# An FFT mixer and an FFN on one core: 47-point steps spread between 64-point steps, weight sums moved to POOL alone in chunks five and six

## The chip, the cores and the metric

One core of a Trainium2 chip runs the whole program. The metric is the device time of one execution in microseconds (us), the median of several runs. The engines are named as in the profile: PE multiplies matrices (PEld loads its weights), DVE and POOL do elementwise work, ACT copies and evaluates functions, SP issues most DMAs. Each engine runs its own instructions in order and waits in order. Tiles are 128 partitions high; POOL works on SBUF alone, and PE's results land in PSUM.

## The reference

```python
X = np.fft.rfft(x, axis=1)                   # x: (8, 3008, 256), real
Xr, Xi = X.real, X.imag
Yr = soft(Xr @ w_r - Xi @ w_i + b_r)         # soft(v) = sign(v) * max(|v| - 0.01, 0)
Yi = soft(Xr @ w_i + Xi @ w_r + b_i)
y = np.fft.irfft(Yr + 1j * Yi, n=3008, axis=1)
t = y.reshape(8 * 3008, 256)                 # 24064 tokens
out = (sigmoid(t @ w_gate) * (t @ w_val)) @ w_out    # d_ff = 1536
```

## The kernel before

**The FFT.** 3008 = 47 x 64. For each batch the forward transform is a 47-point step (`fwd_a`: load x, multiply by `fa`, store z to DRAM), then 64-point steps. A 64-point step `step(q, b)` holds three stages of neighbouring q: `fwd_b` multiplies z by `mf` (tile `pb`), `mix` applies `w_r` and `w_i` (tiles `pm`, then `yt`, `ys`, `yc`), and `inv_b` multiplies by `mi_sb` (tile `pi`) and stores v to DRAM. An inverse unit `inv_a` loads v (tile `vf`), multiplies by `fb` (tile `pia`), and leaves tokens in SBUF for the first nine chunks or writes them to DRAM (`yf` to `yd`). Batches stand in five groups of 1, 1, 2, 2, 2. The 47-point work of batch 0 and 1 comes first, that of the third group (`half_a`) beside chunk 0. Products are made from a rounded part and a rest (`xh` and `xl`, `yh` and `yl`, `hh` and `hl`), so most come as three matmuls.

**The FFN.** Chunks of 512 tokens and 12 units of 128 hidden channels: `ffn1` gives `pg` and `pv` (12 matmuls), then `sg`, `hh`, `hl`, and `ffn2` adds to `po` (6 matmuls). Chunks 0 to 8 run like this, 108 units. The remaining 19 pairs of chunks use a Strassen form with seven products in place of eight, written out by hand under a manual schedule. It needs sums of weight blocks: `make_t` computes them (tiles `tb` and `tr`) and stores them in `td`; `load_t` and `load_t1` bring them back as `th`, `tl` and into `w1h`, `w1l` before the Strassen part.

**What sets the order.** Beside the units of chunks 1 to 8 runs a list `side` of all other steps, each with a weight. Each FFN unit adds `rate` to a sum, and steps are taken from the list while the sum covers their weight. Before, `side` goes group by group: the 64-point steps of group 1; those of group 2 with the inverse units of group 1 spread among them; then for each of the last two groups all its 47-point steps, then its 64-point steps, with the inverse units of the group before spread over both; at last the inverse units of the last group. The result goes through a scheduler that gives each engine a fixed order by priority, readiness and free slots, so that an instruction may stand far ahead of its place in the code. Slots come from rings named by tag: `big` (x, z, raw weights, `tb`, `tr`), `r2k` (rounded parts), `vf` (v).

**Names that the prediction uses.** `xl` L179 is the rest of x, on POOL in `fwd_a` and on DVE in `half_a`; `xh` L178 its rounded part on ACT; `mi_sb` L221 the load of the inverse matrices, issued by POOL; `tr` L495 the copy of the sums on ACT; `hl` L381 the rest of the hidden values on DVE.

Of the kernel before, what the change touches and what calls it, by code (L numbers as in the profile page):

```python
# [9 lines left out]
F32 = mybir.dt.float32  # L10
F32R = mybir.dt.float32r
# [8 lines left out]
R2, R1 = 47, 64  # L20
NK2 = 24
NQ = 2 * NK2
# [4 lines left out]
HW = 512  # L27
FFT_BANKS, L1_BANKS, L2_BANKS = 3, 3, 2

NF2K, NR2K, NLD, NST, NBIG, NME, NVF, NHH, NSG, NYF = 5, 5, 3, 3, 5, 2, 3, 3, 2, 2  # L30
NCB, NTMP, NHP = 10, 9, 12

SIDE_GAP = 14
PRE = 4
WARM = 24
EARLY = 8
NCONV = 5
# [69 lines left out]
def tile_fft_mix_ffn(ctx: ExitStack, tc, x, w_r, w_i, b_r, b_i, w_one, w_out, mf, mi, mis, fa, fa32, fb, out):  # L107
    nc = tc.nc
    B, S, D = x.shape
    P = 128  # L110
# [11 lines left out]
    sub = nc.vector.tensor_sub  # L122
# [8 lines left out]
    p2 = fft.enter_context(tc.tile_pool(name="p2", bufs=2))  # L131
# [4 lines left out]
    def bank(name, tag="fft", bufs=FFT_BANKS):  # L136
        return (psf if tag == "fft" else psl).tile([P, 512], F32, tag=tag, bufs=bufs, name=name)
# [1 line left out]
    def f2k(name):  # L139
        return p2.tile([P, 2, D], F32, tag="f2k", bufs=NF2K, name=name)  # L140

    def r2k(name):
        return p2.tile([P, 2, D], F32R, tag="r2k", bufs=NR2K, name=name)

    fa_sb = cw.tile([2 * R2, 2, 2 * NQ], F32R, name="fa_sb")
    fa32_sb = cw.tile([2 * R2, 2 * NQ], F32, name="fa32_sb")
# [20 lines left out]
            nc.sync.dma_start(xf[lo_:hi_], xv[b, lo_:hi_, 4 * h:4 * h + 4])  # L167
        held["x", b, h] = xf

    def product_a(xi, az, whole, copy, sub_=nc.gpsimd.tensor_sub):  # L170

        pa = bank("pa")[:2 * NQ]
        if whole:
            nc.tensor.matmul(pa, fa32_sb, xi, start=True, stop=True)
        else:
            xh = r2k("xh")[:2 * R2]
            xl = r2k("xl")[:2 * R2]
            nc.scalar.copy(xh, xi)  # L178
            sub_(xl, xi, xh)  # L179
            nc.tensor.matmul(pa, fa_sb[:, 0], xh, start=True, stop=False)  # L180
            nc.tensor.matmul(pa, fa_sb[:, 0], xl, start=False, stop=False)
            nc.tensor.matmul(pa, fa_sb[:, 1], xh, start=False, stop=True)
        copy(az, pa.rearrange("p (h c) -> p h c", h=2))
# [15 lines left out]
    def half_a(b, h, whole):  # L199

        if ("xh", b, h) in held:
            xi = held.pop(("xh", b, h))[:2 * R2]
        else:
            xi = held["x", b, h // 2][:2 * R2, h % 2 * 2:h % 2 * 2 + 2]
        az = p2.tile([P, 2, D], F32, tag="st", bufs=NST, name="azh")[:2 * NQ]
        product_a(xi, az, whole, nc.scalar.copy, sub)
        nc.sync.dma_start(zv[b][:, 2 * h:2 * h + 2], az)


    def load_mf(q):  # L210
# [103 lines left out]


    def load_v(u):
        vf = p3.tile([P, 2, D], F32, tag="vf", bufs=NVF, name="vf")[:2 * NQ]
        b, h = divmod(2 * u, H)
        nc.sync.dma_start(vf, vv[b][:, h:h + 2])
        held["v", u] = vf  # L320
# [79 lines left out]
    def fft_units(bs, full=False):  # L400


        aa = [(b, h) for b in bs for h in range(R1 // 8)]
        ms = {}
        units = []

        def step_a(i):
            if i == 0:
                for k in range(min(PRE, len(aa))):
                    load_a(*aa[k])  # L410
            if i + PRE < len(aa):
                load_a(*aa[i + PRE])
            fwd_a(*aa[i])

        def loads(q, b):
            if b == bs[0]:
                if q == 0:
                    ms[0, 0] = load_mf(0)
                if q + 1 < NP:
                    ms[q + 1, 0] = load_mf(q + 1)  # L420
                if 0 <= q - 1 < NP:
                    ms[q - 1, 1] = load_mi(q - 1, full)
            if q == 0:
                load_b(b, 0)
            if q + 1 < NP:
                load_b(b, q + 1)

        def step(q, b):
            if q or not full:
                loads(q, b)  # L430
            if q < NP:
                fwd_b(b, q, ms[q, 0], full)
            if 0 <= q - 1 < NP:
                (mix4 if full else mix)(b, q - 1)
            if 0 <= q - 2 < NP:
# [47 lines left out]
    def make_t(fp, i):  # L483
        f0, f1 = 2 * fp, 2 * fp + 1
        g = nc.gpsimd
        w = big("tb").rearrange("p (a b) n -> p a b n", a=2)
        b, t = (w[:, a].rearrange("p a (b n) -> p a b n", b=2) for a in range(2))
        g.tensor_add(b, w1h[:, f0:f1 + 1, i], w1l[:, f0:f1 + 1, i])
        t = t.rearrange("p a b n -> p (a b) n")
        g.tensor_sub(t[:, 0], b[:, 1, 0], b[:, 0, 0])  # L490
        g.tensor_sub(t[:, 2], b[:, 1, 1], b[:, 1, 0])
        g.tensor_add(t[:, 1], t[:, 2], b[:, 0, 0])
        g.tensor_sub(t[:, 3], b[:, 0, 1], t[:, 1])
        r = p2.tile([P, 2, 4, P], F32R, tag="big", bufs=NBIG, name="tr")
        nc.scalar.copy(r[:, 0], t)  # L495
        g.tensor_sub(r[:, 1], t, r[:, 0])
        nc.gpsimd.dma_start(td[fp, i].rearrange("p (v a n) -> p v a n", v=2, a=4), r.bitcast(F32))

    def load_t(fp):
# [186 lines left out]
    groups, b0 = [], 0  # L686
# [13 lines left out]
    w1h = const.tile([P, NF, 2, CT, P], F32R, name="w1h")  # L700
    w1l = const.tile([P, NF, 2, CT, P], F32R, name="w1l")
# [73 lines left out]
    second_fft = fft_units(groups[1])[1]  # L775
    third_fft = fft_units(groups[2])[1]
# [24 lines left out]
    p3 = p3s.enter_context(tc.tile_pool(name="p3", bufs=2, side="right", reuse_waits="tile"))  # L801
    load_a(1, na - 1)
    for u in own0:
        load_v(u)
# [11 lines left out]

    side = []
    behind = []  # L820
    for g in groups[1:] + [[]]:
        main = []
        if g:
            main = second_fft if g is groups[1] else third_fft if g is groups[2] else sum(fft_units(g), [])
        m, n = len(main), len(behind)
        for i in range(m):
            side.append(main[i])
            side += behind[i * n // m:(i + 1) * n // m]
        if not g:
            side += behind  # L830
            behind_last = behind
        behind = []
        us = [u for b in g for u in range(b * H // 2, (b + 1) * H // 2) if u >= u0]
        for i, u in enumerate(us):
            def go(i=i, us=us):
                if i == 0:
                    load_v(us[0])
                if i + 1 < len(us):
                    load_v(us[i + 1])
                inv_a(us[i])  # L840
            behind.append((0.9, go))
    n_last = len(behind_last)
    end = len(ffn) - SIDE_GAP
    rate = sum(w for w, _ in side) / (end - NF)
# [1 line left out]
    p4 = None  # L846
    ts = [(fp, i) for fp in range(NH) for i in range(2)]
    for j, u in enumerate(ffn):
        c, f = divmod(j, NF)
        if c == 0:  # L850
            while raws and (f + 1) * nparts > (nparts - len(parts) - len(raws)) * (NF - 3):
                convert()
                if parts:
                    load_part()
        u()
        if c == 0:
            for i in range(f * nb // NF, (f + 1) * nb // NF):
                if i + 2 < nb:
                    load_half(*beside[i + 2])
                half_a(*beside[i], i % 2 == 0)  # L860
        else:
            acc += rate
            if ts and f % 2:
                make_t(*ts.pop(0))
        while side and (acc >= side[0][0] or j >= end):
            acc -= side[0][0]
            side.pop(0)[1]()
            if len(side) == n_last:
                fft.close()
                p4 = ctx.enter_context(tc.tile_pool(name="p4", bufs=1, reuse_waits="tile"))  # L870
                th, tl = (p4.tile([P, NH, 2, 3, P], F32R, name=t) for t in ("th", "tl"))
                prep = list(PREP)
                to_load = list(range(NH))
            if not side:
                psfs.close()
                psg = ctx.enter_context(tc.tile_pool(name="psg", bufs=1, space=bass.MemoryType.PSUM, reuse_waits="tile"))
        if p4 and to_load:
            load_t(to_load.pop(0))
        if c == NPL - 1:
            if f == 0:  # L880
                load_y(0)
# [21 lines left out]
    with tc.manual_schedule():  # L903
# [16 lines left out]
        n = NPR * NH  # L920
# [33 lines left out]
```

## Time and profile before

| | us |
|---|---|
| median of three runs | 2930.84 (2926.06 to 2931.66) |
| the profiled execution | 2931.34 |
| its span | 2929.6 |
| mean granted clock of PE | 0.979 |

| engine | busy us | share of the span | instructions |
|---|---|---|---|
| PE | 2855.9 | 97% | 13972 |
| PEld | 2351.8 | 80% | 13972 |
| DVE | 2074.0 | 71% | 3100 |
| ACT | 1356.6 | 46% | 2375 |
| POOL | 812.2 | 28% | 667 |

The first FFN unit starts at 124 us of the span, chunk 1 at 223 us, and the Strassen part at about 1180 us, from which on PE is busy without a break. The table gives sums over all stages; what each stage waits for is read from windows of the trace. A busy PE includes matmuls that run at half clock.

### The profile page before, as it was taken

How to read it: one execution, taken by the hardware profiler on the slowest of the kernel's cores; microseconds unless marked ns; L12 is line 12 of the kernel's file. 1: busy time of each engine (PE TensorE's matmuls, PEld its weight loads, DVE VectorE, ACT ScalarE, POOL GpSimd, SP SyncE). 2: the span in 40 equal slices, each digit the busy share in tenths (PEclk: the TensorE clock that was granted, in tenths of full speed). 3: DMA queues.
4: the chain of work that ended last, by engine and by line, in shares of the span. 5: the costliest groups of instructions: out<-in, count | busy, mean ns of one | idle time of the engine just before them, and what ended most of it. 6: DMA issues, size and time to landing. Idle time of an engine off the chain costs nothing.

```text
span 2929.6 us, 38731 instructions
## 1 busy us (share of the span) xinstructions
PE 2855.9 (97%) x13972; PEld 2351.8 (80%) x13972; DVE 2074.0 (71%) x3100; ACT 1356.6 (46%) x2375; POOL 812.2 (28%) x667
## 2 busy tenths in 40 slices
PE   8888999999999999999999999999999999999999
PEld 6656898789879977788888888888888888888887
DVE  4766987178539822677777777777777777777776
ACT  4554555545555533344444444444444444444443
POOL 0365001400230000233333333333333333333321
PEclk9889999999989998999999999999999999999999
DMA  9647544664564464000000000000000000000000
GB/s 268 196 158 225 143 129 124 188 186 137 152 197 143 131 196 125 12 29 30 15 15 29 29 29 15 15 29 30 29 15 15 29 29 30 15 15 29 29 15 15
DMA packets 177951, 237.43 MB, mean 81 GB/s; under 512 B 15682, under 2 KB 129152, under 8 KB 177760
## 3 DMA queue, kind: packets, MB, share of 16 engines
q1 hardware_dynamic: 162768, 215.98, 24.0%
q0 software_dynamic: 14896, 18.95, 2.5%
q8 instruction: 110, 1.80, 0.3%
q14 instruction: 81, 0.66, 0.1%
q10 hardware_dynamic: 96, 0.04, 0.0%
HBM read 133.72 MB, written 101.19 MB: 80 GB/s over the span
## 4 chain that ended last, share of the span: by engine, by line
PE 76%; DVE 3%; DMA 2%; issue 1%; ACT 1%; POOL 0%; SPq 0%; DVEq 0%; ACTq 0%; POOLq 0%
PE pd L613 11%; PE pc L613 11%; PE pa L613 11%; PE po L585 7%; PE po L584 7%; PE po L583 7%; PE pb L613 5%; PE pia L336 3%; PE pm L268 2%; DMA vf<-vd 1%; PE pb L234 1%; PE pg L371 1%; PE po L392 1%; PE po L390 1%; PE po L391 1%; PE pg L372 1%
## 5 line engine op out<-in xcount | busy, mean ns | idle before, releaser
L672 POOL TENSOR_TENSOR c<-c,c 128x512 f32<-128x512 f32 x114 | 147.2, 1291 | 810.8 <-DVE c L668 641.0
L585 PE MATMUL po<-hl,w 128*128 128x512 f32 x912 | 362.5, 398 | 0.0
L584 PE MATMUL po<-hh,w 128*128 128x512 f32 x912 | 361.6, 397 | 0.0
L583 PE MATMUL po<-hh,w 128*128 128x512 f32 x912 | 360.8, 396 | 0.0
L613 PE MATMUL pc<-s,w1h 128*128 128x512 f32 x912 | 284.1, 393 | 2.8 <-DVE v L647 2.8
L613 PE MATMUL pa<-a,w1h 128*128 128x512 f32 x912 | 284.6, 394 | 0.5 <-ACT u L639 0.5
L668 DVE TENSOR_TENSOR c<-u,pc 128x512 f32<-128x512 f32 x228 | 156.6, 687 | 115.6 <-PE pc L613 106.8
L643 DVE TENSOR_TENSOR u<-u,pb 128x512 f32<-128x512 f32 x228 | 155.3, 681 | 89.5 <-PE pb L613 62.8
L563 ACT CAST hh<-v 128x512 fp32r<-128x512 f32 x114 | 70.7, 620 | 306.2 <-DVE v L653 306.2
L585 PEld LDWEIGHTS po<-hl,w 128*128 128x128 f32 x912 | 171.5, 188 | 41.9
L583 PEld LDWEIGHTS po<-hh,w 128*128 128x128 f32 x912 | 172.0, 189 | 41.0
L613 PEld LDWEIGHTS pa<-a,w1h 128*128 128x128 f32 x912 | 171.4, 188 | 41.1 <-ACT u L639 0.9
L613 PEld LDWEIGHTS pc<-s,w1h 128*128 128x128 f32 x912 | 170.8, 188 | 41.3 <-DVE v L647 4.0
L567 POOL TENSOR_TENSOR hl<-c,hh 128x512 fp32r<-128x512 f32 x114 | 152.3, 1336 | 186.1 <-ACT hh L563 186.1
L584 PEld LDWEIGHTS po<-hh,w 128*128 128x128 f32 x912 | 171.0, 188 | 40.7
L377 DVE TENSOR_TENSOR sg<-sg,pv 128x512 f32<-128x512 f32 x108 | 74.2, 687 | 174.5 <-PE pv L373 165.0
L221 POOL DMA_DIRECT2D mi_sb<-in_mis_dram x48 | 34.1, 711 | 561.2 <-PE pi L307 527.2
L268 PE MATMUL pm<-w_sb,xsh 128*128 128x256 f32 x1008 | 188.9, 287 | 0.3 <-ACT xsh L250 0.2
L613 PE MATMUL pc<-s,w1l 128*128 128x512 f32 x456 | 177.5, 389 | 0.0
L613 PE MATMUL pa<-a,w1l 128*128 128x512 f32 x456 | 177.2, 389 | 0.0
L674 DVE TENSOR_TENSOR u<-u,pd 128x512 f32<-128x512 f32 x228 | 156.8, 688 | 24.9 <-DVE c L668 0.9
L645 DVE TENSOR_TENSOR v<-u,pd 128x512 f32<-128x512 f32 x228 | 156.8, 688 | 24.4 <-DVE u L643 0.5
(172 smaller groups left out, 7220.6 us busy)
## 6 DMA issues: line engine op xcount, KB each, us to landing
zf<-zd SPq DMA_DIRECT2D x96, 256.0 KB, 3.6
vd<-vz SPq DMA_DIRECT2D x96, 256.0 KB, 3.0
vf<-vd SPq DMA_DIRECT2D x128, 192.0 KB, 3.2
out_dram<-ot SPq DMA_DIRECT2D x94, 256.0 KB, 2.2
ypair<-yd SPq DMA_DIRECT2D x19, 1024.0 KB, 4.8
yd<-yf SPq DMA_DIRECT2D x103, 188.0 KB, 2.9
zd<-az SPq DMA_DIRECT2D x44, 384.0 KB, 3.6
xf<-in_x_dram SPq DMA_DIRECT2D x48, 256.0 KB, 4.3
```

The source lines that it names most:

```text
L268: nc.tensor.matmul(o, l, r, start=(i == 0), stop=(i == len(mms) - 1))
L336: nc.tensor.matmul(pa[:, ct, hh], vf[:, hh, ct * P:(ct + 1) * P], fb_sb[:, :PT], start=True, stop=True)
L567: sub_(hl, h, hh)
L583: nc.tensor.matmul(o, wh, hh, start=(f == 0), stop=False)
L584: nc.tensor.matmul(o, wl, hh, start=False, stop=False)
L585: nc.tensor.matmul(o, wh, hl, start=False, stop=(f == NF - 1))
L613: nc.tensor.matmul(o, l, r, start=not more and l is wh and r is xh, stop=l is wl, skip_group_check=more)
L643: add(u, u, b)
L645: add(v, u, d)
L668: add(c12, u, c)
L672: nc.gpsimd.tensor_mul(c12, g12, c12)
L674: add(u, u, d)
```

## The change

Five things change.

1. `side` is built by `merge`, which places each of several lists evenly between two points of a stretch. The first third of the 47-point steps of the fourth group goes between the 64-point steps of group 1 (from 20% on), the rest between those of the third group (up to 85%), and the 47-point steps of the fifth group between the 64-point steps of the fourth (up to 85%). Inverse units are spread as before, but with weight 0.65 in place of 0.9, so `rate` falls, and v is loaded two units ahead in place of one.
2. `make_t` has no ACT copy any more: POOL makes the rounded part itself, in halves. It is called in the odd units of chunks five and six, not from chunk one on.
3. `load_v` of the units that chunks 1 to 8 transform for themselves uses a slot of its own (`vo`), so the ring of three `vf` serves the others alone.
4. Rings: `r2k` 4 in place of 5 and two slots `a2k` for `xh` and `xl` of `fwd_a`; `big` 4 in place of 5; x is loaded two steps ahead in place of four.
5. `load_t` is called only when `side` is empty, in odd units.

```diff
-NF2K, NR2K, NLD, NST, NBIG, NME, NVF, NHH, NSG, NYF = 5, 5, 3, 3, 5, 2, 3, 3, 2, 2
-NCB, NTMP, NHP = 10, 9, 12
+NF2K, NR2K, NLD, NST, NBIG, NME, NVF, NVO, NHH, NSG, NYF = 5, 4, 3, 3, 4, 2, 3, 1, 3, 2, 2
+NCB, NTMP, NHP, NA2K = 10, 9, 12, 2
-PRE = 4
+PRE = 2
...
     def load_v(u):
-        vf = p3.tile([P, 2, D], F32, tag="vf", bufs=NVF, name="vf")[:2 * NQ]
+        own = 2 * UT <= u * UT < T0
+        vf = p3.tile([P, 2, D], F32, tag="vo" if own else "vf", bufs=NVO if own else NVF, name="vf")[:2 * NQ]
...
-        g.tensor_add(b, w1h[:, f0:f1 + 1, i], w1l[:, f0:f1 + 1, i])
+        for k, f in enumerate((f0, f1)):
+            g.tensor_add(b[:, k], w1h[:, f, i], w1l[:, f, i])
...
-        nc.scalar.copy(r[:, 0], t)
-        g.tensor_sub(r[:, 1], t, r[:, 0])
+        for k in (0, 2):
+            g.tensor_copy(r[:, 0, k:k + 2], t[:, k:k + 2])
+            g.tensor_sub(r[:, 1, k:k + 2], t[:, k:k + 2], r[:, 0, k:k + 2])
...
+    def inverse(g):
         us = [u for b in g for u in range(b * H // 2, (b + 1) * H // 2) if u >= u0]
-            def go(i=i, us=us):
-                if i == 0:
-                    load_v(us[0])
-                if i + 1 < len(us):
-                    load_v(us[i + 1])
-                inv_a(us[i])
-            behind.append((0.9, go))
+        ahead = min(NVF - 1, len(us))
+
+        def go(i):
+            for k in range(ahead if i == 0 else 0):
+                load_v(us[k])
+            if i + ahead < len(us):
+                load_v(us[i + ahead])
+            inv_a(us[i])
+        return [(0.65, lambda i=i: go(i)) for i in range(len(us))]
+
+    def merge(*streams):
+
+        return [u for _, _, u in sorted(((lo + (hi - lo) * (i + 0.5) / len(s), k, u) for k, (s, lo, hi) in
+                                         enumerate(streams) for i, u in enumerate(s)), key=lambda t: t[:2])]
+
+    (a3, q3), (a4, q4) = (fft_units(g) for g in groups[3:])
+    n = len(a3) // 3
+    side = (merge((second_fft, 0, 1), (a3[:n], 0.2, 1)) +
+            merge((third_fft, 0, 1), (a3[n:], 0, 0.85), (inverse(groups[1]), 0, 1)) +
+            merge((q3, 0, 1), (a4, 0, 0.85), (inverse(groups[2]), 0, 1)) +
+            merge((q4, 0, 1), (inverse(groups[3]), 0, 1)))
+    behind_last = inverse(groups[4])
+    side += behind_last
...
-            if ts and f % 2:
+            if ts and c >= 5 and f % 2:
                 make_t(*ts.pop(0))
...
-        if p4 and to_load:
+        if p4 and to_load and not side and f % 2:
             load_t(to_load.pop(0))
```

**The order on ACT around the end of chunk 0.** Before, with `tr` the copy of a weight sum, `azh` and `xh` parts of a 47-point half step, `sg` and `hh` of an FFN unit:

```order
L380 CAST hh_1922<-sg_1919 128x512
L183 COPY azh_1757<-pa_1758 96x512
L495 CAST tr_3151<-tb_3145 128x512
L183 COPY azh_1771<-pa_1772 96x512
L178 CAST xh_1781<-xfh_1754 94x512
L396 COPY ot_2094<-po_1296 128x512
L495 CAST tr_3337<-tb_3331 128x512
L183 COPY azh_1779<-pa_1780 96x512
```

The same place of the changed kernel:

```order
L381 CAST hh_1922<-sg_1919 128x512
L183 COPY azh_1757<-pa_1758 96x512
L183 COPY azh_1771<-pa_1772 96x512
L178 CAST xh_1781<-xfh_1754 94x512
L183 COPY azh_1779<-pa_1780 96x512
L329 CAST yth_1227<-pia_1811 128x2x84
```

The copies of the sums are gone from ACT's queue, there and everywhere.

**The order on POOL at the last weight conversion** (`cv_e`, `w1l`). Before, the sums stand around it, though the code asks for them from chunk 1 on:

```order
L488 TENSOR_TENSOR tb_2870<-w1h_102,w1l_103 128x512
L744 TENSOR_TENSOR cv_e_1715<-raw_1586,w1h_102 128x512
L496 TENSOR_TENSOR tr_2617<-tb_2611,tr_2617 128x512
L745 TENSOR_TENSOR w1l_103<-raw_1586,cv_e_1715 128x512
L497 DMA td_95<-tr_2617 128x1024
L490 TENSOR_TENSOR tb_2870<-tb_2870 128x128
```

The same conversion in the changed kernel:

```order
L747 TENSOR_TENSOR cv_e_1715<-raw_1586,w1h_102 128x512
L748 TENSOR_TENSOR w1l_103<-raw_1586,cv_e_1715 128x512
L179 TENSOR_TENSOR xl_2265<-xf_2253,xh_2264 94x512
L221 DMA mi_sb_2193<-in_mis_dram 128x2x256
L179 TENSOR_TENSOR xl_2274<-xf_2253,xh_2273 94x512
```

In place of the sums, the `xl` of 47-point steps now alternate with the issues of `mi_sb`.

**The order on PE where a run of 47-point steps ended before** (`pa` 47-point, `pia` inverse, `pb` 64-point):

```order
L180 MATMUL pa_5756<-xh_5757,fa_sb_73 96x512
L181 MATMUL pa_5756<-xl_5758,fa_sb_73 96x512
L182 MATMUL pa_5756<-xh_5757,fa_sb_73 96x512
L180 MATMUL pa_5765<-xh_5766,fa_sb_73 96x512
L181 MATMUL pa_5765<-xl_5767,fa_sb_73 96x512
L182 MATMUL pa_5765<-xh_5766,fa_sb_73 96x512
L336 MATMUL pia_5777<-fb_sb_101,vf_5698 128x94 x4
L234 MATMUL pb_5793<-mf_sb_5785,zf_5789 128x128 x4
```

A 47-point step of the changed kernel in chunk 4, behind the `pi` of a 64-point step and beside an FFN unit (`pg`):

```order
L307 MATMUL pi_6545<-yh_6313,mi_sb_6129 128x256
L180 MATMUL pa_6559<-xh_6560,fa_sb_73 96x512
L181 MATMUL pa_6559<-xl_6561,fa_sb_73 96x512
L182 MATMUL pa_6559<-xh_6560,fa_sb_73 96x512
L372 MATMUL pg_6578<-yth_4835,w1h_102 128x512
L373 MATMUL pg_6578<-ytl_4836,w1h_102 128x512
L374 MATMUL pg_6578<-yth_4835,w1l_103 128x512
L180 MATMUL pa_6568<-xh_6569,fa_sb_73 96x512
L372 MATMUL pg_6578<-yth_4835,w1h_102 128x512
L181 MATMUL pa_6568<-xl_6570,fa_sb_73 96x512
```

And on POOL the two `xl` of that step:

```order
L179 TENSOR_TENSOR xl_6561<-xf_6199,xh_6560 94x512
L221 DMA mi_sb_6617<-in_mis_dram 128x2x256
L179 TENSOR_TENSOR xl_6570<-xf_6199,xh_6569 94x512
L179 TENSOR_TENSOR xl_6720<-xf_6356,xh_6719 94x512
```

The second `xl` stands behind an issue that reuses the slot of `mi_sb_6129`, so it waits for the `pi` at the top of the PE rows, and PE has eight matmuls between the two.

More of the change, by code (lines that the diff above doesn't have):

```diff
@@ L140, in f2k, with r2k @@
         return p2.tile([P, 2, D], F32, tag="f2k", bufs=NF2K, name=name)
-    def r2k(name):
-        return p2.tile([P, 2, D], F32R, tag="r2k", bufs=NR2K, name=name)
+    def r2k(name, tag="r2k", bufs=NR2K):
+        return p2.tile([P, 2, D], F32R, tag=tag, bufs=bufs, name=name)
     fa_sb = cw.tile([2 * R2, 2, 2 * NQ], F32R, name="fa_sb")
@@ L168, in load_a, with product_a @@
         held["x", b, h] = xf
-    def product_a(xi, az, whole, copy, sub_=nc.gpsimd.tensor_sub):
+    def product_a(xi, az, whole, copy, sub_=nc.gpsimd.tensor_sub, bufs=("a2k", NA2K)):
         pa = bank("pa")[:2 * NQ]
@@ L175, in product_a @@
         else:
-            xh = r2k("xh")[:2 * R2]
-            xl = r2k("xl")[:2 * R2]
+            xh = r2k("xh", *bufs)[:2 * R2]
+            xl = r2k("xl", *bufs)[:2 * R2]
             nc.scalar.copy(xh, xi)
@@ L205, in half_a @@
         az = p2.tile([P, 2, D], F32, tag="st", bufs=NST, name="azh")[:2 * NQ]
-        product_a(xi, az, whole, nc.scalar.copy, sub)
+        product_a(xi, az, whole, nc.scalar.copy, sub, ())
         nc.sync.dma_start(zv[b][:, 2 * h:2 * h + 2], az)
@@ L815, in tile_fft_mix_ffn @@
     nb, nparts = len(beside), len(parts) + len(raws)
[L819 to L832, printed above, removed]
-        us = [u for b in g for u in range(b * H // 2, (b + 1) * H // 2) if u >= u0]
-        for i, u in enumerate(us):
-            def go(i=i, us=us):
-                if i == 0:
-                    load_v(us[0])
-                if i + 1 < len(us):
-                    load_v(us[i + 1])
-                inv_a(us[i])
-            behind.append((0.9, go))
+    def inverse(g):
+        us = [u for b in g for u in range(b * H // 2, (b + 1) * H // 2) if u >= u0]
+        ahead = min(NVF - 1, len(us))
[17 more added lines that the diff above has]
+    side += behind_last
     n_last = len(behind_last)
```

## The prediction

> **What bounds it now.** I read the page first, then a table of windows over the first 1180 us, then the waits inside the windows that lose time. The page, one digit for each of 40 slices:
>
> ```profile
> PE   8888999999999999999999999999999999999999
> DVE  4766987178539822677777777777777777777776
> PEclk9889999999989998999999999999999999999999
> ```
>
> TensorE is the bound: nine tenths or more nearly everywhere. From slice 17 on (1245 us) nothing is left to take. The slices in which DVE falls to 1, 2 or 3 are the 47-point stretches and the end of the inverse work; PE's clock dips in or beside them. I cut the windows there (us; busy time and count of PE, weight load, DVE, ACT, POOL; granted clock; DMA share):
>
> ```profile
> 150.00:180.00 30.00, 28.10 (x116) 20.19 (x115) 24.35 (x34) 19.67 (x35) 13.71 (x8) 1.00 0.57 174
> ...
> 180.00:200.00 20.00, 14.65 (x61) 10.12 (x60) 15.00 (x18) 9.91 (x18) 16.64 (x19) 1.00 0.46 147
> 200.00:257.00 57.00, 43.91 (x151) 28.14 (x150) 18.19 (x21) 24.11 (x46) 54.34 (x71) 0.82 0.56 190
> 257.00:500.00 243.00, 241.25 (x1632) 217.84 (x1632) 221.40 (x414) 124.14 (x205) 16.84 (x25) 1.00 0.52 144
> 500.00:578.00 78.00, 73.83 (x361) 57.58 (x360) 15.70 (x23) 48.93 (x91) 38.97 (x31) 1.00 0.64 183
> 578.00:602.00 24.00, 19.19 (x90) 17.26 (x91) 4.00 (x7) 8.27 (x15) 2.55 (x2) 0.64 0.75 225
> 602.00:780.00 178.00, 176.24 (x1213) 160.12 (x1213) 148.28 (x274) 93.30 (x161) 15.05 (x18) 1.00 0.52 151
> 780.00:838.00 58.00, 57.68 (x281) 45.34 (x280) 14.02 (x18) 34.99 (x66) 24.45 (x20) 1.00 0.62 176
> 838.00:862.00 24.00, 20.97 (x83) 16.32 (x82) 2.09 (x4) 13.54 (x27) 9.72 (x8) 0.64 0.74 219
> 862.00:1040.00 178.00, 177.49 (x1231) 162.71 (x1230) 150.81 (x277) 90.73 (x153) 7.16 (x10) 1.00 0.48 140
> 1040.00:1075.00 35.00, 32.32 (x188) 27.05 (x186) 6.75 (x10) 11.45 (x23) 0.00 (x0) 1.00 0.78 238
> 1075.00:1130.00 55.00, 47.13 (x227) 41.17 (x226) 4.52 (x8) 12.96 (x27) 0.00 (x0) 0.74 0.60 179
> ```
>
> I call a window's loss its length less PE busy, plus PE busy times (1 - granted clock). It is an upper estimate, since work that waits for data runs no slower at half clock. 180 to 257 loses 5.4 + 13.1 + 43.9 x 0.18 = 26.4 us; 500 to 578 loses 4.2; 578 to 602 loses 4.8 + 19.2 x 0.36 = 11.7; 838 to 862 loses 3.0 + 21.0 x 0.36 = 10.6; 1040 to 1130 loses 2.7 + 7.9 + 47.1 x 0.26 = 22.8. The long 64-point windows lose 1.8, 1.8 and 0.5 us in 599, with DVE as high as 221.4 / 243 = 91%. So a stretch in which PE and DVE are both full costs nothing; the losses sit where work runs out or an in-order queue blocks.
>
> **Weight sums out of 180 to 257 us.** Here POOL is 95% busy with the weight sums, and ACT waits in order for each of them:
>
> ```profile
> DVE xl L179 <- ACT xh L178: 21.7, 6, 5.7
> ACT tr L495 <- POOL tb L493: 20.6, 8, 3.3
> ...
> PE pa L180 <- ACT xh L178: 8.8, 5, 3.7
> ```
>
> The copy `tr` stands in ACT's queue ahead of `xh`, which PE needs for the next half product; the clock then falls to 0.82. After the change neither stands in that place on ACT or POOL. What remains is the pace of 150 to 180, where 1.9 us of 30 were idle: 77 x 0.063 = 4.9 us. The 64-point pipeline of batch 1 still has to fill; I allow 2.5 us, between the 1.8 of the 257 to 500 window and the 4.2 of 500 to 578. Gain 26.4 - 4.9 - 2.5 = 19 us. Bounds: 11 (only the idle of PE goes, 18.4, less those rests) and 22 (only the pace remains).
>
> In their new place the twelve sums are on POOL alone. What they cost it, from 185 to 257 us:
>
> ```profile
> L496 POOL TENSOR_TENSOR tr<-tb,tr 128x512 fp32r<-128x512 f32 x12 | 16.3, 1357 | 0.7 <-ACT tr L495 0.7
> L488 POOL TENSOR_TENSOR tb<-w1h,w1l 128x512 f32<-128x512 f32 x11 | 14.5, 1316 | 0.0
> L491 POOL TENSOR_TENSOR tb<-tb 128x128 f32<-128x128 f32 x12 | 7.8, 652 | 0.0
> L490 POOL TENSOR_TENSOR tb<-tb 128x128 f32<-128x128 f32 x12 | 7.3, 610 | 0.8
> L492 POOL TENSOR_TENSOR tb<-tb 128x128 f32<-128x128 f32 x12 | 6.0, 499 | 0.4
> L493 POOL TENSOR_TENSOR tb<-tb 128x128 f32<-128x128 f32 x12 | 5.9, 495 | 0.9
> ```
>
> That is 57.8 us, 4.9 each. The cast, now on POOL, has no row: between nothing and the 1.36 of the `tr` subtraction of the same size, so 4.9 to 6.2 each; I take the upper end, since a POOL row is the nearest. Nobody waits for the sums before the tail. In the new POOL order they stand within about 13 FFN units (some 130 us): 75 us of POOL, with room for the rest. They do meet DVE, though. The same subtraction, with POOL 95% busy and with POOL nearly free:
>
> ```profile
> L381 DVE TENSOR_TENSOR hl<-sg,hh 128x512 fp32r<-128x512 f32 x8 | 7.6, 951 | 6.3 <-ACT hh L380 6.3
> ...
> L251 DVE TENSOR_TENSOR xsl<-xsf,xsh 128x768 fp32r<-128x768 f32 x35 | 33.3, 953 | 1.4 <-ACT xsh L250 1.1
> L377 DVE TENSOR_TENSOR sg<-sg,pv 128x512 f32<-128x512 f32 x22 | 15.1, 688 | 1.6 <-PE pv L373 0.9
> L381 DVE TENSOR_TENSOR hl<-sg,hh 128x512 fp32r<-128x512 f32 x22 | 15.1, 686 | 0.4
> ```
>
> DVE pays 265 ns. A 64-point step has six DVE operations that read two SBUF tiles, an FFN unit one. Thirteen of each make 91 x 0.265 = 24 us over 130. An FFN unit costs DVE 1.4 us (`sg` and `hl`), a step about 5.4: the 257 to 500 window has some 35 steps and 22 units in its 221.4 us. One of each in 10 us is 6.8; the 24 us bring it from 68% to 87%, still under the 91% that cost nothing. I take 3 us, range 0 to 10.
>
> The Trainium skill, page "SBUF — State Buffer", section "Who interferes with whom", says that VectorE and GpSimd share one port pair by an exclusive lock held for a whole instruction. The rows agree in direction: of `hl`, 951 against 686. By the row the sum stays at 2899; by a full lock, with every meeting paid in full, it would come to the last rival's 2938.
>
> **47-point steps between 64-point steps.** Moved: 32 steps, each with two x loads and one z store on SP, two `xl` on POOL, four copies on ACT and six matmuls. PE's matmuls stay the same in number. What goes is the pair of seams and the thin DVE stretches ahead of them:
>
> ```profile
> PE pb L234 <- DMA zf<-zd: 4.0, 1, 4.0
> PE pia L336 <- DMA vf<-vd: 3.0, 1, 3.0
> ```
>
> At 590 us the first 64-point step waits for z that was just written; with the 47-point steps ending 15% before their stretch, z is old by then. The losses of 500 to 602 and 838 to 862 are 26.5 us. Left are the fills of three group changes at about 1.8 us each. Gain 26.5 - 5.5 = 21 us, range 14 to 24. ACT does not become the bound: 124 of 243 us in the dense window, and four copies of 0.54 us (48.93 / 91) for each 47-point step, of which there is one in some 16 us (32 from 257 to about 790). The x loads run two steps ahead, not four, so about 30 us, against 4.3 us to landing. A z store waits in SP's order for its copy, and loads of z for 64-point steps now stand behind it:
>
> ```profile
> xf<-in_x_dram SPq DMA_DIRECT2D x48, 256.0 KB, 4.3
> ...
> SPq L191 <- ACT az L183: 41.0, 15, 3.9
> ```
>
> That is 2.7 us a time, and a load of z is issued one step, about 5 us or more, ahead of its use; nothing, or the 1 us that I keep in the next term.
>
> New is that `xl` shares POOL's in-order queue with the `mi_sb` issues, which wait for PE to leave a slot:
>
> ```profile
> L179 POOL TENSOR_TENSOR xl<-xf,xh 94x512 fp32r<-94x512 f32 x64 | 81.6, 1287 | 91.1 <-ACT yf L353 47.1 <-PE pa L181 30.6 <-ACT xh L178 5.3
> L221 POOL DMA_DIRECT2D mi_sb<-in_mis_dram x46 | 32.7, 710 | 557.9 <-PE pi L307 527.2 <-PE pg L373 13.5 <-PE pb L234 11.9
> ...
> 1300.00:1350.00 50.00, 50.00 (x218) 40.48 (x217) 39.70 (x55) 20.75 (x36) 16.05 (x12) 1.00 0.00 0
> ```
>
> In the new order eight or nine `xl` stand right behind such an issue, and PE has eight 512-column matmuls (218 in 50 us in the Strassen part, 0.23 each, 1.9 us) between the `pi` that frees the slot and the matmul that reads `xl`. Needed: 0.71 + 1.29 us and hand-overs, about 2.3. So some 0.35 us each, 3 us in all, range 0 to 6. The split of one buffer from `big` moves a `raw` load and one x load later on SP near 65 and 100 us; its nearest row is one load's landing, 4.3 us. It is mostly behind conversions: I take 2, range 0 to 4.
>
> **Tail, 1040 to 1130.** Own `vf` slot, two loads ahead, `load_t` only at odd units. The chain and the waits there:
>
> ```profile
> PE pia L336 <- DMA vf<-vd: 10.1, 13, 2.2
> ...
> 1079.60 5.14 DMA vf<-vd
> 1084.87 1.10 PE pia L336 x8
> 1089.00 4.48 DMA vf<-vd
> ```
>
> Three slots and 4.5 + 1.1 us a turn give one inverse unit per 1.9 us; 32 units take 60 us, whatever the look-ahead, and SP's order still sets `th` and `tl` loads among them. The lower weight (0.65 for 0.9) puts 28 rather than 26 units into the same six FFN units, so a little less covers them. I take no change; bounds -8 (two units at 1.9 us and some clock) and +15 (the 10.1 us of waits and the clock share of them).
>
> **Sum.** 19 + 21 - 3 - 3 - 2 + 0 = 32 us. The profiled execution took 2931.34 us, 1.7 over its span, and 0.5 over the median of three. 2931.3 - 32 = 2899 us. All lower ends together give -3, all upper ones 61; either is unlikely.
>
> **Rivals.** (1) The tail gains as well: the 10.1 us of waits go, and part of the half clock, 13 us together: 2886. For it, the loads come in pairs in the new SP order; against it, the slot count. (2) The seams only move: each of three group changes brings back the 4.0 us wait and its half clock, so that step two gives 5 us in place of 21, and the `mi_sb` issues cost 6: 19 + 5 - 6 - 5 = 13, 2918. For it, the wait at 590 is for a landing, which no order of PE shortens. (3) Nothing happens, 2931: the program's scheduler already moved the sums ahead of their place once and might gather the 47-point steps again; the orders shown speak against it. (4) Slower: POOL holds DVE out. In those 130 us POOL's 79 us and the 91 DVE operations at about 0.65 us exclude each other: 138 us, and with DVE's other 30 us in series 169, 39 over: 2938. It decides from 32 us of loss, that is when each of the 91 pays (40 us of slack + 32) / 91 = 0.79 us, against 0.265 measured.
>
> **Chances.** Forecast 0.56 (2887 to 2911), tail too 0.14, seams move 0.18, nothing 0.05, slower 0.07. What a measurement of this kernel can tell is about 0.2%, 6 us. Faster takes the first three less a little at the edge, 0.86; same 0.06; slower 0.08. The range 2881 to 2922 takes in the first three, but for the far ends of the two side cases.
>
> **What would show it.** Right: 180 to 257 us has no `ACT tr` waits, POOL is thin there, PE's clock 1.00; DVE runs at 60 to 85% through the whole of 260 to 1030 with PE above 98% and no `pb` wait of microseconds; `hl` has a longer mean in chunks five and six. The last part, 1040 to 1130, loses about what it lost. Wrong: PE waits on `POOL xl` of over a microsecond, many times; DVE above 95% in chunks five and six; or a first gate matmul that starts several us later than before's.

## The result, and the profile after

The changed kernel takes 2902.14 us (median of four runs, 2895.31 to 2906.55) against 2931.25: a ratio of 0.990, 95% interval 0.9875 to 0.9925. Four more runs of it (experiment e9) gave 0.9886, 0.9868 to 0.9904; the eight runs together have a median of 2896.2 us. Two executions at a lower mean granted clock, the profiled one of e9 (0.81) and one of e12 (0.875), are left out of all times here. 2899 was forecast. The total is near; the parts are not, as the windows show. The profiled execution took 2903.83 us. First its page, one digit for each of 40 slices:

```profile
PE   9889999999999999999999999999999999999999
DVE  3767778676787833877777777777777777777776
PEclk7899999999999999999999999999999999999999
```

DVE falls below 6 only in slice 0 and in 14 and 15, the end of the inverse work, and PE's clock is low only at the start. The windows at nearly the same cuts as before (us; busy time and count of PE, weight load, DVE, ACT, POOL; granted clock; DMA share; GB/s):

```profile
200.00:257.00 57.00, 55.50 (x271) 41.59 (x271) 32.24 (x53) 30.57 (x54) 5.02 (x4) 1.00 0.57 168
257.00:500.00 243.00, 231.51 (x1455) 200.15 (x1455) 200.20 (x336) 132.26 (x228) 51.07 (x47) 1.00 0.55 155
500.00:578.00 78.00, 73.90 (x465) 63.91 (x464) 55.09 (x94) 40.62 (x72) 15.20 (x13) 1.00 0.55 158
578.00:602.00 24.00, 23.25 (x144) 20.18 (x145) 17.76 (x30) 13.43 (x25) 4.78 (x4) 1.00 0.59 175
602.00:780.00 178.00, 169.75 (x1066) 147.34 (x1065) 125.29 (x201) 95.72 (x169) 51.21 (x56) 1.00 0.56 165
780.00:838.00 58.00, 54.52 (x358) 47.99 (x357) 43.30 (x58) 25.34 (x46) 55.05 (x83) 1.00 0.64 200
838.00:862.00 24.00, 21.26 (x124) 18.68 (x123) 22.46 (x32) 9.16 (x16) 18.64 (x28) 0.93 0.58 190
862.00:1030.00 168.00, 168.00 (x1146) 154.34 (x1145) 133.22 (x239) 84.38 (x142) 7.04 (x10) 1.00 0.48 142
1030.00:1065.00 35.00, 34.12 (x230) 29.92 (x229) 9.49 (x16) 12.78 (x25) 0.00 (x0) 1.00 0.65 192
1065.00:1115.00 50.00, 46.44 (x269) 39.34 (x268) 10.88 (x15) 17.81 (x37) 2.92 (x2) 0.97 0.81 250
```

Where POOL was 95% busy (200 to 257) PE now runs without a dip. The seams are gone: 578 to 602 has PE at 23.25 of 24 us and full clock (19.19 and 0.64 before). But the long windows that lost 1.8 us each, 257 to 500 and 602 to 780, now lose 11.5 and 8.3, spread thinly. PE's waits between 257 and 790 us, in total, count, longest:

```profile
PE pa L181 <- POOL xl L179: 20.8, 31, 0.9
PE pa L180 <- ACT xh L178: 1.1, 3, 0.5
```

and before:

```profile
PE pa L181 <- POOL xl L179: 1.8, 6, 0.4
```

To compare kernels I use one measure per stretch of FFN units: the time from the first gate matmul of one unit to that of a later one, less the nominal time of all matmuls between (0.23 us for 512 columns, 0.12 for 256, 0.11 for the `pb` and `pia` ones), summed over the trace. I call it the loss. The columns from units 0-11 to sum are us of loss, from one profiled execution of each kernel; the nominal times are rounded, so differences under 1 us say nothing. The first column is in us of the span (the recorded expectations put these starts 0.2 us earlier).

| kernel | first gate matmul at | units 0-11 | 12-23 | 24-65 | 66-89 | 90-107 | sum | median time |
|---|---|---|---|---|---|---|---|---|
| before | 124.3 | 32.9 | 18.9 | 26.4 | 15.7 | 27.8 | 121.7 | 2931.3 |
| changed | 133.6 | 19.0 | 13.3 | 31.1 | 12.3 | 9.8 | 85.5 | 2896.2 (8 runs) |
| e1 one ring of six | 134.6 | 18.2 | 14.0 | 52.1 | 20.3 | 11.9 | 116.5 | 2923.9 |
| e2 no vo | 124.7 | 18.8 | 13.4 | 31.2 | 14.6 | 20.3 | 98.3 | 2911.1 |
| e3 no vo, one yf, big 5 | 124.1 | 19.3 | 14.2 | 30.6 | 12.6 | 38.9 | 115.6 | 2927.7 |
| e4 e1 with e3 | 123.7 | 19.6 | 11.4 | 53.0 | 19.2 | 41.5 | 144.7 | 2955.7 |
| e5 no vo, one yf, four slots | 125.4 | 18.1 | 13.9 | 9.8 | 13.6 | 38.0 | 93.4 | 2907.4 |
| e6 xl on DVE | 130.7 | 18.1 | 6.6 | 14.7 | 13.7 | 9.0 | 62.1 | 2871.7 |
| e7 sums as before | 131.0 | 25.7 | 21.1 | 34.5 | 3.9 | 9.3 | 94.5 | 2899.1 |
| e8 sums from chunk 6 | 124.7 | 19.1 | 13.8 | 29.5 | 13.8 | 9.7 | 85.9 | 2894.8 |
| e10 no spread | 124.4 | 18.6 | 7.5 | 55.1 | 51.9 | 11.4 | 144.5 | 2954.5 |
| e11 tail loads as before | 126.4 | 18.3 | 13.3 | 31.2 | 14.0 | 9.1 | 85.9 | 2901.3 |
| e12 xl on DVE, sums from chunk 6 | 123.5 | 19.4 | 6.0 | 13.8 | 9.1 | 14.0 | 62.3 | 2870.8 |

Median less sum lies between 2804 and 2816 us in all thirteen rows, so the sum carries the differences.

### The profile page after: what moved, and what is told of

The parts are those of the page before. It is cut to its first block, busy times and chain, and to the rows that moved or that the text cites. A ratio compares the mean times of both kernels' runs of the same rounds, so it can differ in the third digit from the quotient of the medians.

```text
span 2902.1 us, 38768 instructions
## 1 busy us (share of the span) xinstructions
PE 2832.1 (98%) x13972; PEld 2330.6 (80%) x13972; DVE 2123.4 (73%) x3100; ACT 1347.6 (46%) x2363; POOL 837.9 (29%) x715
## 4 chain that ended last, share of the span: by engine, by line
PE 69%; DMA 1%; DVE 1%; ACT 0%; issue 0%; SPq 0%; DVEq 0%; ACTq 0%
PE pd L616 11%; PE pc L616 11%; PE pa L616 11%; PE po L588 7%; PE po L587 7%; PE po L586 7%; PE pb L616 5%; PE pia L337 2%; PE pm L268 2%; DMA yd<-yf 1%; PE pb L234 1%; PE pg L372 1%; PE pg L373 1%; PE pv L374 1%; PE pg L374 1%; PE po L393 1%
## 5 line engine op out<-in xcount | busy, mean ns | idle before, releaser
L671 DVE TENSOR_TENSOR c<-u,pc 128x512 f32<-128x512 f32 x228 | 156.5, 686 | 115.6 <-PE pc L616 107.2
L650 DVE TENSOR_TENSOR v<-v,pc 128x512 f32<-128x512 f32 x228 | 156.6, 687 | 24.5 <-DVE v L648 0.9
L642 ACT COPY u<-pa 128x512 f32<-128x512 f32 x228 | 133.7, 586 | 79.7 <-PE pa L616 79.7
```

Of the source, the lines that this page charges most:

```text
L650: add(v, v, c)
L671: add(c12, u, c)
```

## The experiments

All edits are to the changed kernel, and every ratio is to the kernel before, on the same chip. The kernel before took 2926.7 to 2931.3 us in the batches of these runs, so times of different batches compare within a few us.

**e1: one ring for all rounded parts.** The theory was that two slots for `xh` and `xl` are too few.

```diff
-NF2K, NR2K, ... = 5, 4, ...
+NF2K, NR2K, ... = 5, 6, ...
-    def product_a(xi, az, whole, copy, sub_=nc.gpsimd.tensor_sub, bufs=("a2k", NA2K)):
+    def product_a(xi, az, whole, copy, sub_=nc.gpsimd.tensor_sub, bufs=()):
```

> The two slots of xh and xl (tag a2k) are put into the ring of yh and yl, which so has six slots: the same memory. Theory A: the spread 47-point steps lose time because xh and xl of one half product hold both slots of the ring until TensorE has read them, so the copy and the subtraction of the second half product (0.62 and 1.29 us) start too late; then TensorE's waits for POOL's xl between 257 and 790 us fall from 20.8 us to under 5 us and the kernel gains 15 to 20 us against the changed kernel (2882 to 2887 us). Theory B (the prediction's step 4): xl is late behind the mi_sb issues in POOL's queue; then the waits stay at 15 to 21 us and the time at 2899 to 2905 us.

2923.89 us, ratio 0.9982 (0.9969 to 0.9994): 28 us slower than the changed kernel, outside both theories. PE's waits for `xl` rose:

```profile
PEld pa L181 <- POOL xl L179: 49.3, 55, 1.3
...
PE pa L181 <- POOL xl L179: 31.4, 55, 0.9
```

A 47-point step has two products, each with its pair `xh` and `xl`. In the changed kernel all 31 waits are for the second pair, and the first lies ready 1.2 to 21 us before its matmul; in e1 most steps wait for both. So an own ring, even a short one, lets the first pair be made early. Why the shared ring did not was not followed further.

**e2: without vo.**

```diff
-        own = 2 * UT <= u * UT < T0
+        own = False
```

> All v tiles go through the ring vf of three, the slot vo is gone, everything else as changed. If the own slot is what made the tail of the FFT (1040 to 1130 us) gain some 17 us, that stretch loses 10 to 17 us again and the time is 2912 to 2919 us. If the tail's gain comes from the later load of the weight sums, from the loads two units ahead or from the smaller weight of an inverse unit, the time stays at 2899 to 2905 us.

2911.09 us, ratio 0.9940 (0.9923 to 0.9957). The losses up to unit 65 are the changed kernel's to a few tenths; units 90 to 107 lose 20.3 instead of 9.8. PE's waits for v from 1020 to 1120 us, first of e2:

```profile
PE pia L337 <- DMA vf<-vd: 6.8, 10, 1.9
```

and of the changed kernel:

```profile
PE pia L337 <- DMA vf<-vd: 0.7, 1, 0.7
```

Before, they were 10.1 us. `vo` is worth 10.5 of the 18 us that the tail gained.

**e3: five big slots.** The room comes from `vo` and one `yf` slot.

```diff
-..., NBIG, ..., NYF = ..., 4, ..., 2
+..., NBIG, ..., NYF = ..., 5, ..., 1
...
-        own = 2 * UT <= u * UT < T0
+        own = False
```

> The ring big has five slots again; the room comes from vo (gone, as in the run before) and from the second yf slot. Theory: the first gate matmul is late (133.4 us, 124.1 before the change) because four x tiles of the second batch fill the ring of four and the az tiles behind them find no slot; then the first gate matmul comes at 123 to 127 us and the kernel is 6 to 10 us faster than the run without vo. Rival: the start varies by itself or is late for another reason; then it stays at 131 to 135 us and the time is that of the run without vo (up to 3 us more, for the single yf slot).

2927.65 us, ratio 0.9994 (0.9983 to 1.0005), 17 us slower than e2. The first gate matmul comes at 124.1 us, but in e2, with four slots, at 124.7: four slots do not make it late. The 17 us are in the tail, where one `yf` slot makes ACT wait for its stores. The waits of 1020 to 1120 us, first of e3:

```profile
ACT yf L354 <- DMA yd<-yf: 38.3, 18, 3.6
...
PE pia L337 <- ACT yf L354: 15.9, 16, 3.0
```

and of the changed kernel:

```profile
ACT yf L354 <- DMA yd<-yf: 19.7, 14, 3.0
...
PE pia L337 <- ACT yf L354: 3.6, 4, 1.7
```

So the tail's next bound, once v is there in time, is the store of `yf`.

**e4: e1 and e3 together.**

> Both at once: one ring of six for xh, xl, yh and yl, and big with five slots (no vo, one yf slot). If both causes hold and add up, the gain against the changed kernel is 15 to 20 us from the xl waits and 6 to 10 us from the start, less what the missing vo costs (0 to 17 us): 2872 to 2895 us. If neither holds, 2900 to 2920 us.

2955.67 us, ratio 1.0089 (1.0076 to 1.0102). Neither cause held, and the time is above both ranges: the table's row is e1's middle with e3's tail.

**e5: four own slots.** `vo` and one `yf` slot are gone as in e3, so the tail is that of e3; `big` stays at four.

```diff
-..., NYF = ..., 2
+..., NYF = ..., 1
-NCB, NTMP, NHP, NA2K = 10, 9, 12, 2
+NCB, NTMP, NHP, NA2K = 10, 9, 12, 4
...
-        own = 2 * UT <= u * UT < T0
+        own = False
```

> The own ring of xh and xl gets four slots instead of two; the room comes from vo (gone) and from the second yf slot, which the runs e2 and e3 showed to touch only what follows 1020 us. Between the gate matmuls of units 18 and 66 the run e2 lost 29.5 us (sum of the blocks). Theory A, mended: the first product's pair holds both slots, so the second product's xl is late (31 waits, 20 us of TensorE); sharing the ring of yh and yl cured nothing because it took the early pair away as well. Then with four own slots the waits for POOL's xl fall under 6 us, the stretch loses 12 to 20 us less, and the time is 2907 to 2915 us (e3, with the same tail, has 2927.7). Rival C: the scheduler sets TensorE's order by its own durations, and puts L181 too close behind xh whatever the slots are; then the waits stay at 18 to 32 us and the time at 2923 to 2932 us.

2907.43 us, ratio 0.9924 (0.9904 to 0.9944), 20 us faster than e3, as theory A said. Units 18 to 65 lose 14.0 us against e2's 36.7 (the 29.5 in the expectation was a wrong sum). PE's waits between 247 and 790 us begin with

```profile
PE pi L305 <- ACT yh L279: 2.0, 4, 0.9
PE pi L305 <- ACT xsf L246: 1.8, 2, 1.1
```

and have no `xl` row. POOL still waits with its `mi_sb` issues for 118 + 78 us there, as in the changed kernel (115 + 85). That alone would not clear the queue behind those issues, since four slots give slack to hide it. The changed kernel's trace does: in 30 of its 31 late products the `xl` starts within 0.1 us of the end of its `xh`, so POOL had waited for ACT and not for an issue, and in 25 of them that `xh` started within 0.1 us of the matmul that read the first `xl`. The slots were the cause. One such product (start, length, and in brackets the wait and its releaser):

```profile
442.43 0.62 ACT L178 CAST xh<-xf 94x512 fp32r<-94x512 f32 x1 [0.26 <-PE pa L181]
...
443.14 1.29 POOL L179 TENSOR_TENSOR xl<-xf,xh 94x512 fp32r<-94x512 f32 x1 [1.39 <-ACT xh L178]
...
443.33 1.39 DVE L257 TENSOR_SCALAR yc<-ys 128x512 f32<-128x512 f32 x1
...
444.49 0.48 PE L181 MATMUL pa<-xl,fa_sb 94*96 94x512 f32 x1 [0.68 <-POOL xl L179]
```

The second `xh` starts when PE has read the first `xl` and so freed its slot; then ACT's 0.62 us and POOL's 1.29 us follow one another, and PE has less than that to do before it needs the second `xl`.

**e6: xl on DVE.**

```diff
-    def product_a(xi, az, whole, copy, sub_=nc.gpsimd.tensor_sub, ...
+    def product_a(xi, az, whole, copy, sub_=nc.vector.tensor_sub, ...
```

> xl of the 47-point steps is made by DVE instead of POOL, nothing else. POOL's subtraction takes 1.26 to 1.29 us, DVE's of 128x512 0.69 us. If TensorE's waits for xl (20.8 us between 257 and 790 us) come from the length of that operation, they fall to under 8 us, and the time to 2888 to 2895 us. Rival: DVE, 82% busy between 257 and 500 us, takes 64 operations of 0.69 us more and is then late for xsl, ys and yl: TensorE waits for pm, pi and pb by as much as it gains, 2900 to 2910 us.

2871.65 us, ratio 0.9794 (0.9774 to 0.9814): 25 us faster than the changed kernel, and faster than both expectations: more than the waits alone. PE's wait for `xl` between 257 and 790 us:

```profile
PE pa L181 <- DVE xl L179: 2.8, 9, 0.7
```

DVE did not become late: its own operations became shorter, as POOL no longer works beside them. DVE's groups from 257 to 500 us (count, busy us and mean ns), changed kernel:

```profile
L275 DVE TENSOR_TENSOR ys<-yt 64x256 f32<-64x256 f32 x56 | 28.2, 504 | 1.3
...
L258 DVE TENSOR_TENSOR yc<-ys,yc 128x512 f32<-128x512 f32 x28 | 23.3, 831 | 0.8
L280 DVE TENSOR_TENSOR yl<-yc,yh 128x512 fp32r<-128x512 f32 x29 | 22.4, 771 | 5.5 <-ACT yh L279 5.1
L270 DVE TENSOR_TENSOR yt<-pm,bias_sb 128x512 f32<-128x512 f32 x27 | 18.6, 690 | 5.0 <-PE pm L268 4.8
...
L257 DVE TENSOR_SCALAR yc<-ys 128x512 f32<-128x512 f32 x28 | 13.8, 492 | 0.6
```

and e6:

```profile
L275 DVE TENSOR_TENSOR ys<-yt 64x256 f32<-64x256 f32 x58 | 24.4, 421 | 1.2
...
L270 DVE TENSOR_TENSOR yt<-pm,bias_sb 128x512 f32<-128x512 f32 x29 | 20.0, 689 | 4.5 <-PE pm L268 4.2
L258 DVE TENSOR_TENSOR yc<-ys,yc 128x512 f32<-128x512 f32 x29 | 19.9, 688 | 0.5
L280 DVE TENSOR_TENSOR yl<-yc,yh 128x512 fp32r<-128x512 f32 x29 | 19.9, 687 | 2.7 <-ACT yh L279 2.4
L179 DVE TENSOR_TENSOR xl<-xf,xh 94x512 fp32r<-94x512 f32 x29 | 19.9, 686 | 3.9 <-ACT xh L178 2.0 <-PE pb L234 1.4
...
L257 DVE TENSOR_SCALAR yc<-ys 128x512 f32<-128x512 f32 x28 | 11.8, 421 | 0.3
```

The four slowed groups give back 56 x 0.083 + 28 x 0.143 + 29 x 0.084 + 28 x 0.071 = 13 us, so 19.9 us of `xl` cost DVE 7 net.

**e7: the weight sums as before.**

```diff
-            if ts and c >= 5 and f % 2:
+            if ts and f % 2:
...
-        for k in (0, 2):
-            g.tensor_copy(r[:, 0, k:k + 2], t[:, k:k + 2])
-            g.tensor_sub(r[:, 1, k:k + 2], t[:, k:k + 2], r[:, 0, k:k + 2])
+        nc.scalar.copy(r[:, 0], t)
+        g.tensor_sub(r[:, 1], t, r[:, 0])
```

> The weight sums go back to chunks one and two, with ScalarE's copy, as before the change; the rest as changed. The prediction's step 1 put 19 us on their removal from 180 to 257 us, the blocks of units 6 to 17 suggest 14; step 2 put 3 us on their arrival in chunks five and six, the traces suggest 8. So by the prediction this run is 16 us slower than the changed kernel (2918 us), by the traces 6 us (2908 us); units 66 to 77 lose 8 us less than the 11.2 us they lose there. Rival: the sums cost 15 us before only because they met the 47-point steps of the same stretch; those have moved, and the run is within 3 us of the changed kernel.

2899.12 us, ratio 0.9900 (0.9880 to 0.9920). Units 0 to 65 lose 17.9 us more than in the changed kernel (one half-clock window of 6.8 us in units 24 to 29 among them), units 66 to 89 lose 8.4 less. The profiled execution, the slowest of its six, is 7 us slower than the changed kernel's; the median is 3 slower than that of eight runs, with intervals of 6 us on either side. So the net of moving the sums is not told apart from nothing by the times, as the rival said, though in the traces both halves are there, with a net of 9 us. The run does not bring the old place back: its sums start on POOL from 193 to 480 us, those of the kernel before from 182 to 249 us. So it prices sums spread from the end of chunk zero over chunks one and two of the changed kernel. DVE from 780 to 860 us, changed kernel:

```profile
L382 DVE TENSOR_TENSOR hl<-sg,hh 128x512 fp32r<-128x512 f32 x7 | 7.8, 1116 | 2.1 <-ACT hh L381 2.1
...
L280 DVE TENSOR_TENSOR yl<-yc,yh 128x512 fp32r<-128x512 f32 x6 | 7.3, 1213 | 1.4 <-ACT yh L279 1.4
...
L248 DVE TENSOR_TENSOR xsf<-xsf 128x256 f32<-128x256 f32 x7 | 7.0, 998 | 4.7 <-ACT xsf L246 4.6
...
L257 DVE TENSOR_SCALAR yc<-ys 128x512 f32<-128x512 f32 x7 | 4.9, 700 | 0.2
L378 DVE TENSOR_TENSOR sg<-sg,pv 128x512 f32<-128x512 f32 x7 | 4.8, 688 | 3.5 <-PE pv L374 3.4
```

and e7:

```profile
L280 DVE TENSOR_TENSOR yl<-yc,yh 128x512 fp32r<-128x512 f32 x8 | 5.8, 721 | 3.5 <-ACT yh L279 3.5
...
L378 DVE TENSOR_TENSOR sg<-sg,pv 128x512 f32<-128x512 f32 x8 | 5.5, 687 | 6.5 <-PE pv L374 6.3
L382 DVE TENSOR_TENSOR hl<-sg,hh 128x512 fp32r<-128x512 f32 x7 | 4.8, 692 | 2.9 <-ACT hh L381 2.7
...
L257 DVE TENSOR_SCALAR yc<-ys 128x512 f32<-128x512 f32 x8 | 3.4, 428 | 0.3
L248 DVE TENSOR_TENSOR xsf<-xsf 128x256 f32<-128x256 f32 x7 | 3.0, 423 | 5.7 <-ACT xsf L246 5.7
```

**e8: the sums later.**

```diff
-            if ts and c >= 5 and f % 2:
+            if ts and c >= 6 and f % 3:
```

> The weight sums on POOL start in chunk six (two units out of three) instead of five, so they lie between 856 and 1010 us, where POOL is 4% and DVE 79% busy. If what they cost is the stretch 795 to 862 us, where DVE is over 80% busy beside them, units 66 to 71 lose 8 us less (9.8 in the changed kernel), units 72 to 89 lose 0 to 4 us more, and the time is 2893 to 2898 us. Rival: POOL slows DVE as much in the later place and the loss moves along: 2900 to 2906 us. On the other side: the big slots that the sums hold in chunk seven delay x tiles or the end of the FFT's memory: 2906 to 2912 us.

2894.76 us, ratio 0.9877 (0.9858 to 0.9896): no difference from the changed kernel that is clear of the noise. The time lies in the expected range, but by chance: the run did not test the place. The scheduler took the sums forward, to 770 to 864 us of its trace (723 to 851 in the changed kernel's), and units 66 to 89 lose 13.8 us as before. Whether they would be free after 864 us stays open.

**e9: the changed kernel once more.**

> The changed kernel word for word, for more runs of it: its four runs lie between 2895.3 and 2906.6 us, and the profiled one held TensorE at half clock from 18.4 to 45.7 us, the profiled runs e2, e3, e5 and e8 for 3 to 10 us there only, with the same order of instructions at the start in e2, e5 and e8. If the first gate matmul at 133.4 us (124.1 before) is such a chance of the start and not the work of the change, it comes at 124 to 126 us in some executions of this same kernel, and the median is 2896 to 2902 us. If the ring of four does it, it comes at 131 to 135 us.

2894.4 us (four executions), ratio 0.9886 (0.9868 to 0.9904). Its own trace is left out, but the other kernels' traces bear on the question. In all ten traces with four `big` slots, from the changed kernel and e1, e2, e5 to e8 and e10 to e12, the order on PE is the same until after the first gate matmul. It comes at 123.5 to 126.4 us in e2, e5, e8, e10, e11 and e12, and at 130.7 to 134.6 in the changed kernel, e1, e6 and e7. The difference is a stretch at half clock. Window 18 to 46 us of the changed kernel:

```profile
18.00:46.00 28.00, 27.26 (x38) 10.04 (x39) 7.56 (x12) 9.24 (x17) 0.00 (x0) 0.51 0.82 242
```

and of e11:

```profile
18.00:46.00 28.00, 21.30 (x66) 10.92 (x67) 8.83 (x14) 11.88 (x23) 0.00 (x0) 0.88 0.92 283
```

The instructions are the same; 38 matmuls ran in the one and 66 in the other. So the ring of four does not by itself make the start late. What sets the half clock off in some executions stays open. The three traces with five slots (before, e3, e4) do not have a stretch of this length, which is too few to say whether the change makes it more frequent.

**e10: without the spread.**

```diff
-    side = (merge((second_fft, 0, 1), (a3[:n], 0.2, 1)) +
-            ...
+    for g in groups[1:] + [[]]:
+        ...
```

> The side list is put together as before the change (the 47-point steps of a group in a row, ahead of its 64-point steps), the rest as changed. By the prediction's steps 3 and 4 the spread is worth 21 less 3 us, so this run takes 2917 to 2922 us. By the traces it gave back nearly all at once: the seams' 26 us returned, and the waits for POOL's xl took some 22 us; then this run takes 2898 to 2908 us, with two stretches of 47-point steps where DVE is under 50% busy and TensorE loses 10 us each, and the waits for xl elsewhere under 5 us.

2954.51 us, ratio 1.0098 (1.0080 to 1.0117), 58 us slower than the changed kernel and 28 slower than the kernel before on the same chip. Both expectations were far too low. Windows of e10 over the 47-point steps of the fourth group, and what follows:

```profile
500.00:560.00 60.00, 53.25 (x242) 38.84 (x240) 13.49 (x16) 29.98 (x58) 21.80 (x17) 1.00 0.55 156
560.00:607.00 47.00, 33.32 (x130) 26.31 (x130) 6.73 (x11) 15.13 (x29) 21.11 (x29) 0.53 0.59 182
```

PE's waits from 500 to 607 us begin with

```profile
PE pa L181 <- POOL xl L179: 9.3, 17, 0.9
PE pa L180 <- ACT xh L178: 6.7, 7, 2.0
```

and from 560 us on the clock halves. The kernel before had its 47-point steps in the same place of the list, with `xh` and `xl` in the ring of five, and waited 1.8 us for `xl` from 257 to 790 us. So with the short own ring, two loads ahead and four `big` slots, 47-point steps in a row are dear, and the spread pays for that. The waits are for `xl` and `xh`, and no engine waits there for an x load, so the trace points to the ring; none of the three was tried alone.

**e11: the tail's loads as before.**

```diff
-        ahead = min(NVF - 1, len(us))
+        ahead = min(1, len(us))
...
-        if p4 and to_load and not side and f % 2:
+        if p4 and to_load:
```

> The tail's loads as before: v tiles one unit ahead instead of two, and the weight sums loaded at once instead of at every second unit after the side list; vo stays. The own slot vo was worth 11 us of the tail's 17 (run e2). If these two parts are the rest, the blocks of units 90 to 101 lose 5 to 8 us more than the changed kernel's 9.3 us, and the time is 2902 to 2908 us; if the smaller weight of an inverse unit or chance is the rest, they lose the same within 2 us, 2896 to 2902 us.

2901.32 us, ratio 0.9914 (0.9897 to 0.9931): the median is inside the spread of the eight runs, though all six executions are above e9's four on the same chip. In the traces units 90 to 107 lose 9.1 us against 9.8, and the sums of all units agree within 1 us, so no worth of the two parts shows. The 7.5 us of the tail's gain that `vo` does not explain are left to the weight of an inverse unit and the merged order, which were not tried alone.

**e12: e6 and e8 together.**

> xl of the 47-point steps on DVE (run e6) and the weight sums from chunk six on (run e8), the rest as changed. If the two gains add up: 2871.7 less 3 to 8 us, 2862 to 2869 us. If DVE, which then has the xl of the 47-point steps but not the sums beside them, already hid the sums' cost, 2869 to 2873 us.

2870.8 us (four executions), ratio 0.9802 (0.9784 to 0.9820), the same as e6. Both beat the kernel before by 2% and the changed one by 25 us; the later sums add nothing to the time. In its trace units 66 to 89 lose 4.6 us less than in e6, and units 90 to 107 lose 5.0 more, where PE ran 10.2 us at half clock; one trace each does not say whether that belongs to the edit.

## Why the prediction was right in its total, and where not

**Sums out of 180 to 257 us: held.** 19 us forecast; units 0 to 23 lose 19.5 us less than before. The mechanism is the forecast one: PE's 8.8 us of waits for `xh` from 200 to 257 us are gone, and the window 200 to 257 runs at full clock. In e7, with the sums back in chunks one and two, these units lose 14.5 us more.

**Sums against DVE: the price was too low.** 3 us taken, 8.4 measured (e7), inside the range. The 265 ns came from `hl` alone. Here `hl` pays 424 (692 to 1116 ns), `xsf` 575, `yl` 490, and `yc` L257, which has one SBUF input and was not counted, 270. The scheduler also packed the sums, so POOL is 95% busy in 780 to 838 us. The last rival's loss of 39 us did not come about; its 2938 added the 39 to a sum that had taken 3 of them already, and should have been 2935.

**The spread, the xl behind it: the step that failed.** For units 24 to 89 the forecast was a gain of 15 us: 21 for the spread, less 3 for `xl` and 3 for the sums. They lost 42.1 us before and 43.4 after: nothing. The seams went much as forecast, the loss of 500 to 602 and 838 to 862 from 26.5 to 9.1 us. But the term for `xl` looked for its price in POOL's queue, behind `mi_sb`; it lay in the ring of two, which the working did not price at all. Four slots give 21 us back (units 24 to 65, e2 to e5). With them units 24 to 89 lose 23.4 us, 18.7 less than before: the spread's own gain was forecast about right, and the ring ate it. The sign that was named for it, waits of over a microsecond, was wrong too: there were 31 of 0.67 on average.

**big from five to four: nothing.** 2 us forecast; e2 with four slots starts its first gate matmul 0.6 us after e3 with five. The 9.3 us by which the profiled execution starts it later than before come with its half clock at 18 to 46 us. So the late first gate matmul, which the prediction named as a sign of being wrong, does not speak against it.

**Tail: rival 1 came true.** No change forecast, 18 us gained, past the bound of 15. The working took three slots for one turn of 1.9 us per unit; the slot that the chunks' own units had held in that ring was counted as none. It was worth 10.5; what the other 7.5 belong to stays open.

So 32 us forecast came out as 19.5 - 1.3 + 18 = 36 by the table, less the 9.3 us of the start in the profiled execution. The total is right by luck: two errors of 16 and 18 us cancelled. Of the signs of being right, a busy PE "above 98%" through 260 to 1030 failed (95% from 257 to 780), and DVE left its 60 to 85% in 838 to 862 (94%).

## What to carry to other kernels

A ring whose slots one product fills makes the next product's preparation wait for the matmuls of this one: count slots in whole products. Sharing the ring with other tiles was no cure: it cost 28 us here. Before handing an operation to an idle POOL, price what it does to DVE's operations on SBUF beside it: here 0.69 us on a DVE that was 82% busy was cheaper than 1.29 us on a POOL at 21%. When a reordering and a smaller ring come in one change, price the ring first in the old order.

## What the runs showed of the hardware

An operation of POOL can hold up DVE's work on SBUF nearly to its own end: at 443.33 us above, `yc` L257 (0.42 us in e6) takes 1.39 us and ends 0.3 us after POOL's `xl`. Operations with an input in PSUM did not pay here: `yt` took 690 ns beside POOL's `xl` and 689 without it (e6), `sg` 688 beside the sums and 687 without them (e7). The Trainium skill, page "SBUF — State Buffer", section "Who interferes with whom", has the rule: an exclusive lock on a shared port pair, taken by DVE operations with two SBUF inputs and by some forms of `copy`, `cast` and `tensor_scalar`. These rows agree with it; the prediction counted only the first kind. Not expected either was a half clock of 27.3 us, with PE busy for 27.26 of 28 us, that comes in four traces and stays away in six with the same order on PE up to there.
